# Two buffers for transposed rows, plain logits, held-back output scatters, and expert slots that start one unit later, in a convolution with routed experts

## The chip, the cores and the metric

The kernel runs on one core of one Trainium2 chip. The metric is the time on the device in microseconds (us).

## The reference, cut to what matters

```python
B, S, D, H, K = 8, 3584, 192, 8, 7           # 28672 rows of 192
N, E, F = B * S, 8, 1024
w = softmax(weight)                          # (H, K): one causal 7-tap filter per head
x = causal_conv(x, w).reshape(N, D)
logits = x @ w_gate                          # (N, E)
e_idx  = argmax(logits, axis=1)              # each row goes to one expert
gate_w = softmax(logits)[arange(N), e_idx]
eom    = sigmoid(x @ w_output_gate)
for e in range(E):
    mask = e_idx == e
    out[mask] = gate_w[mask, None] * eom[mask, e, None] * (relu(x[mask] @ w1[e]) @ w2[e])
```

## The kernel before

The rows are worked through in 16 units of 1792. A unit's front convolves the rows, computes 16 logits per row, picks an expert, and scatters the rows, pair by pair, into one stream per expert in DRAM. A slot is the expert work on 512 rows of one expert's stream: it is loaded with two transposing DMAs (xa, xb), multiplied with w1, put through a ReLU, multiplied with w2 and scattered to the output. While the slots of unit u run, in steps q = 0 to 3 each, generators `front_a(u + 2)` and `front_b(u + 1)` lay the fronts of later units between their products.

```python
pxt = ctx.enter_context(tc.tile_pool(name="pxt", bufs=6))       # xa, xb
...
NXS = 6                                                         # buffers of the stream scatters
...
# front_a: the logits, four products at a time in four column tiles
pl = pft()
for i in range(2):
    for g in range(4):
        nc.tensor.matmul(pl[32 * g:32 * g + 32, 0:4 * BT],
                         wg[:, (g // 2) * 2 + i, :],
                         tt[:, g // 2 + i, (g % 2) * 4 * BT:(g % 2 + 1) * 4 * BT],
                         start=(i == 0), stop=(i == 1), tile_position=(0, 32 * g))
...
def plan(u):                      # four slots a unit, of one half of the experts; eight in the last
    if u == 0:
        return []
    p = plan_half((u + 1) % 2, "a")
    if u == NU - 1:
        p += plan_half(u % 2, "b")
    return p
...
# Slot.second, at the end of each pair of steps: one stream scatter, then one output scatter
            for j in (q - 1, q):
                emit_in()
                i = nc.gpsimd.indirect_dma_start(out=out, out_offset=..., in_=self.y[:, j, :], ...)
...
for u in range(1, NU):            # main part
    todo = []
    for e, bap, inv in plans.pop(u):
        base = reg(bap, [ET.SP], E * CAP - TT)
        todo.append((e, inv, slot_load(base, u)))
    fa = front_a(u + 2) if u + 2 < NU else iter(())
    fb = front_b(u + 1) if u + 1 < NU else iter(())
    for k, (e, inv, xab) in enumerate(todo):
        s = Slot(xab, w_at(e * WE), inv)
        for q in range(4):
            s.first(q)
            drain(fa, 1)
            if prev is not None:
                prev.second(q)
            drain(fb, 1)
        prev = s
    ...
with tc.For_i(0, rn, 1):          # a loop takes what is left, one slot per turn
    ...
```

Of the kernel before, what the change touches and what calls it, by code (L numbers as in the profile page):

```python
# [11 lines left out]
FP16 = mybir.dt.float16  # L12
# [9 lines left out]
def kernel(  # L22
# [10 lines left out]
    nc = tc.nc  # L33
# [26 lines left out]
    WE = F + F + FCH * D  # L60
    BIG = float(1 << 30)
# [10 lines left out]
    pxt = ctx.enter_context(tc.tile_pool(name="pxt", bufs=6))  # L72
# [65 lines left out]
    wg = const.tile([128, 4, 32], FP32)  # L138
    nc.vector.memset(wg, 0.0)
    for i, (p0, p1, d0) in enumerate([(0, 128, 0), (0, 64, 128), (64, 128, 0), (0, 128, 64)]):  # L140
        nc.scalar.dma_start(wg[p0:p1, i, 0:E], moe_w_gate[d0:d0 + p1 - p0, :])
        nc.scalar.dma_start(wg[p0:p1, i, E:2 * E], moe_w_output_gate[d0:d0 + p1 - p0, :])
# [50 lines left out]
    NXS = 6  # L193
# [7 lines left out]
    nc.vector.tensor_copy(out=pos16, in_=poi.rearrange("p r j -> p (r j)"))  # L201

# [43 lines left out]

    wres = const.tile([128, E * WE], FP16)

    def load_w(e):
        o = e * WE  # L250
        nc.gpsimd.dma_start(wres[:, o:o + F], moe_w1[e, 0:128, :])
        nc.gpsimd.dma_start(wres[0:64, o + F:o + 2 * F], moe_w1[e, 128:D, :])
        nc.gpsimd.dma_start(
            wres[:, o + 2 * F:o + WE].rearrange("p (c d) -> p c d", d=D),
            moe_w2[e].rearrange("(c p) d -> p c d", p=128))

# [28 lines left out]
    def front_a(u):  # L285
# [12 lines left out]
        tt = pct.tile([128, 3, NB // 2 * BT], FP32, tag="tt", name="tt")  # L298
        cvf = cv.rearrange("p c d -> p (c d)")
        for g in range(6):  # L300
            pt = pft()
            for j in range(4):
                m, i = (g // 3) * 4 + j, g % 3
                nc.tensor.matmul(pt[:, j * BT:(j + 1) * BT],  # L304
                                 cvf[0:BT, m * 2 * D + i * 128:m * 2 * D + (i + 1) * 128],
                                 identf[0:BT, 0:BT],
                                 is_transpose=True, start=(j == 0), stop=(j == 3))
            evac(tt[:, g % 3, (g // 3) * 4 * BT:(g // 3 + 1) * 4 * BT], pt[:, 0:4 * BT])
            yield
        pl = pft()  # L310
        for i in range(2):
            for g in range(4):
                nc.tensor.matmul(pl[32 * g:32 * g + 32, 0:4 * BT],
                                 wg[:, (g // 2) * 2 + i, :],
                                 tt[:, g // 2 + i, (g % 2) * 4 * BT:(g % 2 + 1) * 4 * BT],
                                 start=(i == 0), stop=(i == 1), tile_position=(0, 32 * g))
        lt = pct.tile([128, 4 * BT], FP32, tag="lt", name="lt")
        evac(lt, pl[:, 0:4 * BT])
        yield
        pg = pft()  # L320
        for j in range(4):
            nc.tensor.matmul(pg[0:BT, j * 128:(j + 1) * 128],
                             lt[:, j * BT:(j + 1) * BT], identf,
                             is_transpose=True, start=(j == 0), stop=(j == 3))
        gb = pr.tile([128, NB, 16], FP32, tag="gb", name="gb")

        nc.vector.tensor_copy(
            out=gb[0:BT].rearrange("p (l i) e -> p i l e", l=2),
            in_=pg[0:BT].rearrange("p (i l e) -> p i l e", l=2, e=32)[:, :, :, 0:16])
# [140 lines left out]

    def nodep(i, group, others):
        inst = i.ins if hasattr(i, "ins") else i
        for o in others:
            tc.declare_no_dep(inst, group=o, reason="distinct rows of the stream or output")
        tc.add_to_no_dep_group(group, inst)
# [27 lines left out]

    def plan(u):
        if u == 0:
            return []
# [240 lines left out]
```

## Time and profile before

| | kernel before |
|---|---|
| timed runs | 806.73 us median of 3 (802.25 to 811.64) |
| profiled run | 773.92 us, span 772.0 |
| TensorE busy | 655.4 us, 85% of the span |
| TensorE waiting for the transposed load of a slot | 73.3 us |
| a full unit (first product of its first slot to that of the next unit) | 43.2 us |

The lines behind these numbers are shown in the prediction.

### The profile page before, as it was taken

How to read it: one execution, taken by the hardware profiler on the slowest of the kernel's cores; microseconds unless marked ns; L12 is line 12 of the kernel's file. 1: busy time of each engine (PE TensorE's matmuls, PEld its weight loads, DVE VectorE, ACT ScalarE, POOL GpSimd, SP SyncE). 2: the span in 40 equal slices, each digit the busy share in tenths (PEclk: the TensorE clock that was granted, in tenths of full speed). 3: DMA queues.
4: the chain of work that ended last, by engine and by line, in shares of the span. 5: the costliest groups of instructions: out<-in, count | busy, mean ns of one | idle time of the engine just before them, and what ended most of it. 6: DMA issues, size and time to landing. Idle time of an engine off the chain costs nothing. (4 is left out here: it accounts for less than half of the span.)

```text
span 772.0 us, 14134 instructions
## 1 busy us (share of the span) xinstructions
PE 655.4 (85%) x4948; PEld 436.2 (57%) x4948; DVE 406.5 (53%) x1298; ACT 366.5 (47%) x581; POOL 411.5 (53%) x425
## 2 busy tenths in 40 slices
PE   3866498989989898989989898989989898869953
PEld 1524165665757475656747475656757575547632
DVE  7425183836566383837556383837566474802220
ACT  0657153554535363545536364545546354436621
POOL 1436145473747465473737465563737375656652
PEclk9978599999999999999999999999999999989987
DMA  7999933253535343252535343442532313234110
GB/s 152 231 238 203 142 101 108 72 160 75 144 102 143 103 133 104 69 155 73 152 92 139 99 127 106 101 133 62 157 88 74 93 61 110 70 102 114 48 41 9
DMA packets 132359, 86.59 MB, mean 112 GB/s; under 512 B 88427, under 2 KB 122455, under 8 KB 132288
## 3 DMA queue, kind: packets, MB, share of 16 engines
q1 hardware_dynamic: 102656, 42.35, 23.4%
q0 software_dynamic: 28736, 43.31, 20.5%
q8 instruction: 39, 0.64, 0.4%
q14 instruction: 32, 0.26, 0.1%
q10 hardware_dynamic: 896, 0.03, 0.1%
HBM read 35.80 MB, written 44.43 MB: 104 GB/s over the span
## 5 line engine op out<-in xcount | busy, mean ns | idle before, releaser
L579 POOL DMA_INDIRECT out_dram<-y,oi x260 | 262.7, 1011 | 242.1 <-issue 179.0
L547 ACT ACTIVATE ht<-pp 128x1024 f16<-128x1024 f32 x195 | 199.3, 1022 | 183.9 <-PE pp L541 183.9
L539 PE MATMUL pp<-xa,wres 128*128 128x512 f16 x520 | 203.0, 390 | 61.1 <-DMA xa<-xcg_sorted 61.1
L558 PE MATMUL pyt<-wres,ht 128*128 128x192 f16 (+1 forms) x2080 | 220.9, 250 | 2.9 <-DVE ht L545 2.9
L558 PEld LDWEIGHTS <-ht 128*128 128x128 f16 x2080 | 182.7, 99 | 67.1 <-issue 37.0
L541 PE MATMUL pp<-xb,wres 128*128 128x512 f16 x520 | 202.2, 389 | 12.2 <-DMA xb<-xcg_sorted 12.2
L457 POOL DMA_INDIRECT xcg_sorted<-xs,du x128 | 130.1, 1017 | 89.4 <-ACT xs L278 42.2
L290 PE MATMUL pf<-xt,band 118*112 118x384 f32 x256 | 115.3, 543 | 19.5 <-DMA xt<-in_x_dram 14.1
L539 PEld LDWEIGHTS <-wres 128*128 128x128 f16 (+1 forms) x520 | 51.4, 99 | 112.4 <-DMA xa<-xcg_sorted 41.2
L545 DVE TENSOR_SCALAR ht<-pp 128x1024 f16<-128x1024 f32 x65 | 79.2, 1219 | 59.2 <-PE pp L541 59.2
L569 ACT COPY y<-pyt 128x384 f32<-128x384 f32 x130 | 62.4, 480 | 93.9 <-PE pyt L558 84.1
L280 DVE COPY cv<-pf 112x384 f32<-112x384 f32 x54 | 29.2, 541 | 89.3 <-PE pf L290 89.3
L290 PEld LDWEIGHTS pf<-xt,band 118*112 118x112 f32 x256 | 48.0, 195 | 48.9 <-DVE band L133 13.6
L541 PEld LDWEIGHTS <-wres 128*128 128x128 f16 (+1 forms) x520 | 51.8, 100 | 37.6 <-issue 8.2
L572 DVE TENSOR_SCALAR oi<-pyt 128x4 uint32<-128x4 f32 x65 | 10.5, 162 | 115.8 <-ACT y L569 110.3
L439 PE MATMUL pf<-xrow,pm 112*128 112x194 f16 x512 | 64.6, 247 | 6.9 <-DVE pm L423 4.5
L418 DVE TENSOR_TENSOR xrow<-cv,gs 112x384 f16<-112x384 f32 x128 | 64.7, 545 | 0.0
L423 DVE TENSOR_SCALAR pm<-pos,pos 112x256 f16<-112x256 f16 x256 | 64.6, 324 | 0.0
L304 PEld LDWEIGHTS pf<-identf,cv 112*128 112x128 f32 x384 | 43.6, 141 | 17.4 <-DVE cv L280 2.2
L278 ACT COPY cv<-pf 112x384 f32<-112x384 f32 x74 | 33.9, 479 | 40.1 <-PE pf L290 25.0
L304 PE MATMUL pf<-identf,cv 112*128 112x112 f32 x384 | 51.5, 260 | 0.5 <-ACT cv L278 0.4
L278 ACT CAST xs<-pf 128x388 f16<-128x388 f32 x76 | 37.2, 489 | 28.8 <-PE pf L439 20.2
(132 smaller groups left out, 425.0 us busy)
## 6 DMA issues: line engine op xcount, KB each, us to landing
xt<-in_x_dram SPq DMA_DIRECT2D x8, 1344.0 KB
xt<-in_x_dram SPq DMA_DIRECT2D x8, 1260.0 KB
out_dram<-y,oi POOLq DMA_INDIRECT x260, 2.7
wres<-in_moe_w_dram POOLq DMA_DIRECT2D x8, 384.0 KB, 10.5
wres<-in_moe_w_dram POOLq DMA_DIRECT2D x8, 256.0 KB, 11.5
xcg_sorted<-zrow SPq DMA_DIRECT2D x8, 256.0 KB
xcg_sorted<-xs,du POOLq DMA_INDIRECT x128, 3.2
xa<-xcg_sorted SPq DMA_TRANSPOSE x65
```

The lines of the kernel that those rows point to most:

```text
L278: nc.scalar.copy(out=o, in_=i)
L290: nc.tensor.matmul(pc[0:BT, 0:NB * GH], band[0:KI, h, :], xt[0:KI, :, h * GH:(h + 1) * GH], start=True, stop=True)
L304: nc.tensor.matmul(pt[:, j * BT:(j + 1) * BT], cvf[0:BT, m * 2 * D + i * 128:m * 2 * D + (i + 1) * 128], identf[0:BT, 0:BT], is_transpose= ...
L418: nc.vector.tensor_tensor(out=xr[P, k:k + 2, 0:D], in0=cv[P, k:k + 2, :], in1=gs[P, k:k + 2].unsqueeze(2).to_broadcast([BT, 2, D]), op=ALU ...
L423: nc.vector.tensor_scalar(out=pms[i][P, l, :], in0=pos16[P], scalar1=pos[P, l * NG + i:l * NG + i + 1], scalar2=None, op0=ALU.is_equal)
L457: i = nc.gpsimd.indirect_dma_start(out=xcg2, out_offset=bass.IndirectOffsetOnAxis(ap=du[:, i:i + 1], axis=0), in_=xs.rearrange("p r w -> p ...
L539: nc.tensor.matmul(pp[:, j, :], self.w(fc * 128, 128), self.xa, start=True, stop=False)
L541: nc.tensor.matmul(pp[:, j, :], self.w(F + fc * 128, 128), self.xb, start=False, stop=True)
L545: nc.vector.tensor_relu(out=ht, in_=pp)
L547: nc.scalar.activation(out=ht, in_=pp, func=AF.Relu)
L558: nc.tensor.matmul(self.pp[:, o:o + D], self.ht[fc // 2][:, fc % 2, q * 128:(q + 1) * 128], self.w(2 * F + fc * D, D), start=(fc == 0 and ...
L579: i = nc.gpsimd.indirect_dma_start(out=out, out_offset=bass.IndirectOffsetOnAxis(ap=self.oi[:, j:j + 1], axis=0), in_=self.y[:, j, :], in_ ...
```

## The change

The intent: take away the wait for the load at every unit's start by sending the stream scatters at once and holding the output scatters back; shorten the end by replacing the loop with three slots of the fullest experts; and simplify two things that seemed to have slack (buffers, logits). Beside the core of the diff below, the expert weights are loaded two experts at a time along the front-only units, and the two halves of the experts change places in `plan`. The core:

```diff
-    pxt = ctx.enter_context(tc.tile_pool(name="pxt", bufs=6))
+    pxt = ctx.enter_context(tc.tile_pool(name="pxt", bufs=2))
-    NXS = 6
+    NXS = 12
...
-        for i in range(2):
-            for g in range(4):
-                nc.tensor.matmul(pl[32 * g:32 * g + 32, 0:4 * BT], ..., tile_position=(0, 32 * g))
...
+        for hh in range(2):
+            ...
+            for i in range(3):
+                nc.tensor.matmul(pl[0:32, 0:4 * BT], wg[:, i, :], tt[:, i, cs],
+                                 start=(i == 0), stop=(i == 2))
+            evac(lt[:, cs], pl[0:32, 0:4 * BT])
+        for m in range(NG):                    # eight transposes of 32 rows for four of 128
+            nc.tensor.matmul(pg[0:BT, m * 32:(m + 1) * 32], lt[:, m * BT:(m + 1) * BT],
+                             identf[0:32, 0:32], is_transpose=True, ...)
...
+    U0 = 2
-        if u == 0:
+        if u < U0:
             return []
...
-                for j in (q - 1, q):
-                    emit_in()
-                    i = nc.gpsimd.indirect_dma_start(out=out, ...)
+                pout.extend((self.y, self.oi, j) for j in (q - 1, q))
...
-    for u in range(1, NU):
+    for u in range(U0, NU):
...
+        if u == NU - 1:
+            for sel, bap, inv in [pick() for _ in range(ND)]:      # ND = 3
+                base = reg(bap[0:1, 0:1], [ET.SP], E * CAP - TT)
+                todo.append((sel, inv, slot_load(base, u)))
...
-                drain(fb, 1)
+                live = drain(fb, 1)
+                pos = 4 * k + q
+                emit_in(len(pend))
+                emit_out(5 if live and pos > 3 else 0)
```

More of the change, by code (lines that the diff above doesn't have):

```diff
@@ L60 @@
     WE = F + F + FCH * D
+    ND = 3
     BIG = float(1 << 30)
@@ L136 @@
                 data=cw[:, h:h + H // 2, k:k + 1].to_broadcast([128, H // 2, BT]))
-    wg = const.tile([128, 4, 32], FP32)
+    wg = const.tile([128, 3, 32], FP32)
     nc.vector.memset(wg, 0.0)
-    for i, (p0, p1, d0) in enumerate([(0, 128, 0), (0, 64, 128), (64, 128, 0), (0, 128, 64)]):
-        nc.scalar.dma_start(wg[p0:p1, i, 0:E], moe_w_gate[d0:d0 + p1 - p0, :])
-        nc.scalar.dma_start(wg[p0:p1, i, E:2 * E], moe_w_output_gate[d0:d0 + p1 - p0, :])
+    for i, c, p0, p1, d0 in ((0, 0, 0, 128, 0), (1, 0, 0, 64, 128), (1, 16, 64, 128, 0),
+                             (2, 16, 0, 128, 64)):
+        nc.scalar.dma_start(wg[p0:p1, i, c:c + E], moe_w_gate[d0:d0 + p1 - p0, :])
+        nc.scalar.dma_start(wg[p0:p1, i, c + E:c + 2 * E], moe_w_output_gate[d0:d0 + p1 - p0, :])
     ltri = const.tile([128, 128], FP16)
@@ L201, with load_w @@
     nc.vector.tensor_copy(out=pos16, in_=poi.rearrange("p r j -> p (r j)"))
+    wres = const.tile([128, E * WE], FP16)
+    def load_w(e):
+        o = e * WE
+        nc.gpsimd.dma_start(wres[:, o:o + F], moe_w1[e, 0:128, :])
+        nc.gpsimd.dma_start(wres[0:64, o + F:o + 2 * F], moe_w1[e, 128:D, :])
+        nc.gpsimd.dma_start(
+            wres[:, o + 2 * F:o + WE].rearrange("p (c d) -> p c d", d=D),
+            moe_w2[e].rearrange("(c p) d -> p c d", p=128))
+    load_w(0)
     GE = NG * E
@@ L244 @@
     nc.vector.memset(zrow, 0.0)
-    wres = const.tile([128, E * WE], FP16)
-    def load_w(e):
-        o = e * WE
-        nc.gpsimd.dma_start(wres[:, o:o + F], moe_w1[e, 0:128, :])
-        nc.gpsimd.dma_start(wres[0:64, o + F:o + 2 * F], moe_w1[e, 128:D, :])
-        nc.gpsimd.dma_start(
-            wres[:, o + 2 * F:o + WE].rearrange("p (c d) -> p c d", d=D),
-            moe_w2[e].rearrange("(c p) d -> p c d", p=128))
     def zero_w(e):
@@ L298, in front_a @@
         tt = pct.tile([128, 3, NB // 2 * BT], FP32, tag="tt", name="tt")
+        lt = pct.tile([32, NB // 2 * BT], FP32, tag="lt", name="lt")
         cvf = cv.rearrange("p c d -> p (c d)")
-        for g in range(6):
-            pt = pft()
-            for j in range(4):
-                m, i = (g // 3) * 4 + j, g % 3
-                nc.tensor.matmul(pt[:, j * BT:(j + 1) * BT],
-                                 cvf[0:BT, m * 2 * D + i * 128:m * 2 * D + (i + 1) * 128],
-                                 identf[0:BT, 0:BT],
-                                 is_transpose=True, start=(j == 0), stop=(j == 3))
-            evac(tt[:, g % 3, (g // 3) * 4 * BT:(g // 3 + 1) * 4 * BT], pt[:, 0:4 * BT])
-            yield
@@ L310, in front_a @@
-        pl = pft()
-        for i in range(2):
-            for g in range(4):
-                nc.tensor.matmul(pl[32 * g:32 * g + 32, 0:4 * BT],
-                                 wg[:, (g // 2) * 2 + i, :],
-                                 tt[:, g // 2 + i, (g % 2) * 4 * BT:(g % 2 + 1) * 4 * BT],
-                                 start=(i == 0), stop=(i == 1), tile_position=(0, 32 * g))
-        lt = pct.tile([128, 4 * BT], FP32, tag="lt", name="lt")
-        evac(lt, pl[:, 0:4 * BT])
-        yield
+        for hh in range(2):
+            cs = slice(hh * 4 * BT, (hh + 1) * 4 * BT)
+            for i in range(3):
+                pt = pft()
+                for j in range(4):
+                    o = (hh * 4 + j) * 2 * D + i * 128
+                    nc.tensor.matmul(pt[:, j * BT:(j + 1) * BT], cvf[0:BT, o:o + 128],
+                                     identf[0:BT, 0:BT],
+                                     is_transpose=True, start=(j == 0), stop=(j == 3))
+                evac(tt[:, i, cs], pt[:, 0:4 * BT])
+                if not (hh == 1 and i == 1):
+                    yield
+            pl = pft()
+            for i in range(3):
+                nc.tensor.matmul(pl[0:32, 0:4 * BT], wg[:, i, :], tt[:, i, cs],
+                                 start=(i == 0), stop=(i == 2))
+            evac(lt[:, cs], pl[0:32, 0:4 * BT])
+            yield
@@ L320, in front_a @@
         pg = pft()
-        for j in range(4):
-            nc.tensor.matmul(pg[0:BT, j * 128:(j + 1) * 128],
-                             lt[:, j * BT:(j + 1) * BT], identf,
-                             is_transpose=True, start=(j == 0), stop=(j == 3))
+        for m in range(NG):
+            nc.tensor.matmul(pg[0:BT, m * 32:(m + 1) * 32], lt[:, m * BT:(m + 1) * BT],
+                             identf[0:32, 0:32],
+                             is_transpose=True, start=(m == 0), stop=(m == NG - 1))
@@ L325, in front_a @@
         gb = pr.tile([128, NB, 16], FP32, tag="gb", name="gb")
-        nc.vector.tensor_copy(
-            out=gb[0:BT].rearrange("p (l i) e -> p i l e", l=2),
-            in_=pg[0:BT].rearrange("p (i l e) -> p i l e", l=2, e=32)[:, :, :, 0:16])
+        nc.vector.tensor_copy(out=gb[0:BT],
+                              in_=pg[0:BT, 0:NB * 16].rearrange("p (c e) -> p c e", e=16))
         units[u] = cv, gb
@@ L469, in emit_in, with emit_out @@
             n -= 1
+    pout = deque()
+    def emit_out(keep=0):
+        while len(pout) > keep:
+            y, oi, j = pout.popleft()
+            i = nc.gpsimd.indirect_dma_start(
+                out=out, out_offset=bass.IndirectOffsetOnAxis(ap=oi[:, j:j + 1], axis=0),
+                in_=y[:, j, :], in_offset=None, bounds_check=N - 1, oob_is_err=False)
+            nodep(i, "out", ("out",))
+            last[0] = "out"
     def nodep(i, group, others):
@@ L502, in plan_half, with pick @@
         return [(e0 + i, bu[0:1, i:i + 1], iu[:, i, :]) for i in range(EH)]
+    U0 = 2
     def plan(u):
-        if u == 0:
+        if u < U0:
             return []
-        p = plan_half((u + 1) % 2, "a")
+        p = plan_half(u % 2, "a")
         if u == NU - 1:
-            p += plan_half(u % 2, "b")
+            p += plan_half((u + 1) % 2, "b")
         return p
+    def pick():
+        lv = pr.tile([128, E], FP32, tag="lv", name="lv")
+        nc.vector.tensor_tensor(out=lv, in0=R, in1=DN, op=ALU.subtract)
+        lm = pr.tile([128, 1], FP32, tag="lm", name="lm")
+        nc.vector.tensor_reduce(out=lm, in_=lv, axis=AX.X, op=ALU.max)
+        oh = pr.tile([128, E], FP32, tag="oh", name="oh")
+        nc.vector.scalar_tensor_tensor(out=oh, in0=lv, scalar=lm, in1=rev,
+                                       op0=ALU.is_equal, op1=ALU.mult)
+        om = pr.tile([128, 1], FP32, tag="om", name="om")
+        nc.vector.tensor_reduce(out=om, in_=oh, axis=AX.X, op=ALU.max)
+        sel = pr.tile([128, 1], U32, tag="sel", name="sel", bufs=ND)
+        nc.vector.tensor_scalar(out=sel, in0=om, scalar1=-float(WE), scalar2=float(E * WE),
+                                op0=ALU.mult, op1=ALU.add)
+        nc.vector.tensor_scalar(out=oh, in0=oh, scalar1=om, scalar2=None, op0=ALU.is_equal)
+        bt = pr.tile([128, E], FP32, tag="bt", name="bt")
+        nc.vector.scalar_tensor_tensor(out=bt, in0=R, scalar=-float(TP), in1=DN,
+                                       op0=ALU.add, op1=ALU.min)
+        nc.vector.scalar_tensor_tensor(out=bt, in0=bt, scalar=2.0, in1=oh,
+                                       op0=ALU.mult, op1=ALU.mult)
+        bo = pr.tile([128, 1], FP32, tag="bo", name="bo")
+        nc.vector.tensor_reduce(out=bo, in_=bt, axis=AX.X, op=ALU.add)
+        bou = pr.tile([128, 1], U32, tag="bou", name="bou", bufs=ND)
+        nc.vector.tensor_copy(out=bou, in_=bo)
+        tk1 = pr.tile([128, 1], FP32, tag="tk1", name="tk1")
+        nc.vector.tensor_scalar(out=tk1, in0=lm, scalar1=float(TP), scalar2=None, op0=ALU.min)
+        nc.vector.scalar_tensor_tensor(out=DN, in0=oh, scalar=tk1, in1=DN,
+                                       op0=ALU.mult, op1=ALU.add)
+        nc.vector.tensor_scalar(out=tk1, in0=tk1, scalar1=-2.0, scalar2=float(TT),
+                                op0=ALU.mult, op1=ALU.add)
+        iv1 = pr.tile([128, 4], FP32, tag="iv1", name="iv1")
+        nc.vector.tensor_scalar(out=iv1, in0=rowf, scalar1=tk1, scalar2=BIG,
+                                op0=ALU.is_lt, op1=ALU.mult)
+        iu1 = pr.tile([128, 4], U32, tag="iu1", name="iu1", bufs=ND)
+        nc.vector.tensor_copy(out=iu1, in_=iv1)
+        return sel, bou, iu1
@@ L576, in second @@
                                             op=ALU.bitwise_or)
-                for j in (q - 1, q):
-                    emit_in()
-                    i = nc.gpsimd.indirect_dma_start(
-                        out=out, out_offset=bass.IndirectOffsetOnAxis(
-                            ap=self.oi[:, j:j + 1], axis=0),
-                        in_=self.y[:, j, :], in_offset=None,
-                        bounds_check=N - 1, oob_is_err=False)
-                    nodep(i, "out", ("out",))
-                    last[0] = "out"
+                pout.extend((self.y, self.oi, j) for j in (q - 1, q))
     def reg(ap, engines, hi):
@@ L609, in chain @@
             yield from g
-    for e in range(EH):
-        load_w(e)
+    load_w(1)
     drain(front_a(0))
     ze = 0
-    for u in range(2):
+    for u in range(U0 + 1):
         fa, fb = front_a(u + 1), front_b(u)
@@ L626 @@
         emit_in(len(pend))
-        if u == 0:
-            for e in range(EH, EH + 2):
-                load_w(e)
+        if u < U0:
+            load_w(2 + 2 * u)
+            load_w(3 + 2 * u)
     while ze < E:
@@ L639 @@
             base = reg(bap, [ET.SP], E * CAP - TT)
-            todo.append((e, inv, slot_load(base, u)))
+            todo.append((w_at(e * WE), inv, slot_load(base, u)))
+        if u == NU - 1:
+            for sel, bap, inv in [pick() for _ in range(ND)]:
+                base = reg(bap[0:1, 0:1], [ET.SP], E * CAP - TT)
+                todo.append((sel, inv, slot_load(base, u)))
         fa = front_a(u + 2) if u + 2 < NU else iter(())
         fb = front_b(u + 1) if u + 1 < NU else iter(())
-        for k, (e, inv, xab) in enumerate(todo):
-            if u == 1 and k < 2:
-                load_w(EH + 2 + k)
-            s = Slot(xab, w_at(e * WE), inv)
+        for k, (w, inv, xab) in enumerate(todo):
+            if u == U0 and k < 2:
+                load_w(E - 2 + k)
+            if not callable(w):
+                w = w_dyn(reg(w[0:1, 0:1], [ET.PE], (E - 1) * WE))
+            s = Slot(xab, w, inv)
             for q in range(4):
@@ L658 @@
         prev.second(q)
+        emit_out()
     lf = const.tile([128, E], FP32)
@@ L676 @@
     with tc.For_i(0, rn, 1):
-        lv = pr.tile([128, E], FP32, tag="lv", name="lv")
-        nc.vector.tensor_tensor(out=lv, in0=R, in1=DN, op=ALU.subtract)
-        lm = pr.tile([128, 1], FP32, tag="lm", name="lm")
-        nc.vector.tensor_reduce(out=lm, in_=lv, axis=AX.X, op=ALU.max)
-        oh = pr.tile([128, E], FP32, tag="oh", name="oh")
-        nc.vector.scalar_tensor_tensor(out=oh, in0=lv, scalar=lm, in1=rev,
-                                       op0=ALU.is_equal, op1=ALU.mult)
-        om = pr.tile([128, 1], FP32, tag="om", name="om")
-        nc.vector.tensor_reduce(out=om, in_=oh, axis=AX.X, op=ALU.max)
-        sel = pr.tile([128, 1], U32, tag="sel", name="sel")
-        nc.vector.tensor_scalar(out=sel, in0=om, scalar1=-float(WE), scalar2=float(E * WE),
-                                op0=ALU.mult, op1=ALU.add)
-        nc.vector.tensor_scalar(out=oh, in0=oh, scalar1=om, scalar2=None, op0=ALU.is_equal)
-        bt = pr.tile([128, E], FP32, tag="bt", name="bt")
-        nc.vector.scalar_tensor_tensor(out=bt, in0=R, scalar=-float(TP), in1=DN,
-                                       op0=ALU.add, op1=ALU.min)
-        nc.vector.scalar_tensor_tensor(out=bt, in0=bt, scalar=2.0, in1=oh,
-                                       op0=ALU.mult, op1=ALU.mult)
-        bo = pr.tile([128, 1], FP32, tag="bo", name="bo")
-        nc.vector.tensor_reduce(out=bo, in_=bt, axis=AX.X, op=ALU.add)
-        bou = pr.tile([128, 1], U32, tag="bou", name="bou")
-        nc.vector.tensor_copy(out=bou, in_=bo)
-        tk1 = pr.tile([128, 1], FP32, tag="tk1", name="tk1")
-        nc.vector.tensor_scalar(out=tk1, in0=lm, scalar1=float(TP), scalar2=None, op0=ALU.min)
-        nc.vector.scalar_tensor_tensor(out=DN, in0=oh, scalar=tk1, in1=DN,
-                                       op0=ALU.mult, op1=ALU.add)
-        nc.vector.tensor_scalar(out=tk1, in0=tk1, scalar1=-2.0, scalar2=float(TT),
-                                op0=ALU.mult, op1=ALU.add)
-        iv1 = pr.tile([128, 4], FP32, tag="iv1", name="iv1")
-        nc.vector.tensor_scalar(out=iv1, in0=rowf, scalar1=tk1, scalar2=BIG,
-                                op0=ALU.is_lt, op1=ALU.mult)
-        iu1 = pr.tile([128, 4], U32, tag="iu1", name="iu1")
-        nc.vector.tensor_copy(out=iu1, in_=iv1)
+        sel, bou, iu1 = pick()
         base = reg(bou[0:1, 0:1], [ET.SP], E * CAP - TT)
@@ L716 @@
             s.second(q)
+            emit_out()
 _INS = ['x', 'weight', 'moe_w_gate', 'moe_w_output_gate', 'moe_w1', 'moe_w2']
```

## The prediction

> **What bounds the kernel now.** I read the page first, then the table of stretches cut at the stages, then the waits, then the order of time around one stage boundary.
>
> The first view is the page, engine totals and the slices of the span.
>
> ```profile
> PE 655.4 (85%) x4948; PEld 436.2 (57%) x4948; DVE 406.5 (53%) x1298; ACT 366.5 (47%) x581; POOL 411.5 (53%) x425
> PE   3866498989989898989989898989989898869953
> PEclk9978599999999999999999999999999999989987
> ```
>
> TensorE is at 8 to 9 tenths from slice 6 to slice 38 and loses time at both ends; no other engine passes 53%. The chain of waits has only the last output scatter in it, so it doesn't help. The second view is the table of stretches (columns: length, busy time and count for PE, PEld, DVE, ACT, POOL, granted clock, DMA share, GB/s).
>
> ```profile
> 28.40:47.90 19.50, 14.57 (x101) 8.87 (x99) 13.70 (x52) 11.83 (x25) 6.67 (x7) 1.00 1.20 254
> 47.90:75.90 28.00, 19.32 (x98) 10.30 (x98) 11.98 (x50) 17.48 (x33) 14.15 (x17) 0.76 1.00 223
> 86.10:129.90 43.80, 38.05 (x270) 24.05 (x271) 26.47 (x81) 20.23 (x31) 19.87 (x20) 0.92 0.50 114
> 216.90:259.10 42.20, 38.67 (x307) 26.33 (x307) 23.35 (x73) 21.34 (x34) 24.57 (x25) 1.00 0.43 119
> 647.60:687.30 39.70, 29.20 (x247) 20.07 (x248) 20.41 (x72) 17.77 (x26) 24.31 (x25) 0.96 0.30 90
> 687.30:742.10 54.80, 54.16 (x452) 37.64 (x452) 13.06 (x29) 31.82 (x41) 31.12 (x33) 0.97 0.30 76
> 742.10:772.00 29.90, 10.65 (x52) 5.26 (x52) 4.78 (x23) 4.50 (x6) 8.45 (x9) 0.73 0.09 24
> ```
>
> The first two rows are the front-only units (no expert products yet), the second of them slow. The third is the first unit with slots (a slot: 512 rows of one expert). The fourth is a typical unit at full clock: 38.67 us of TensorE work in 42.2 us, so about 3.5 us of idle. Then come the unit with half of the front, the last eight slots, and the loop at the end: 29.9 us with 10.65 of TensorE work, for a single slot. The thirteen units from 86.1 to 647.6 take (647.6 - 86.1)/13 = 43.2 us each. The third view, the waits, says what the idle is.
>
> ```profile
> PE pp L539 <- DMA xa<-xcg_sorted: 61.1, 16, 13.4
> PE pp L541 <- DMA xb<-xcg_sorted: 12.2, 16, 2.5
> SPq L516 <- DMA xcg_sorted<-xs,du: 253.0, 32, 20.2
> ```
>
> 73.3 us of the 116.6 us that TensorE is idle are waits for the transposed load of a stage's first slot, and that load waits for the stage's scatters. The fourth view is TensorE in order of time at one boundary, the fifth GpSimd at the same place.
>
> ```profile
> 122.96 1.71 PE L313 MATMUL pf<-tt,wg 128*32 128x448 f32 x16
> 124.61 0.83 PE L558 MATMUL pyt<-wres,ht 128*128 128x192 f16 x8
> 126.14 0.60 PE L322 MATMUL pf<-identf,lt 128*112 128x128 f32 x4
> 126.58 0.82 PE L558 MATMUL pyt<-wres,ht 128*128 128x192 f16 x8
> 129.93 0.38 PE L539 MATMUL pp<-xa,wres 128*128 128x512 f16 x1 [2.53 <-DMA xa<-xcg_sorted]
> 130.77 0.38 PE L541 MATMUL pp<-xb,wres 128*128 128x512 f16 x1 [0.46 <-DMA xb<-xcg_sorted]
> ```
>
> ```profile
> 122.78 0.98 POOL L579 DMA_INDIRECT out_dram<-y,oi  x1 [0.30 <-issue]
> 124.07 0.98 POOL L457 DMA_INDIRECT xcg_sorted<-xs,du  x1 [0.30 <-issue]
> 125.36 0.98 POOL L579 DMA_INDIRECT out_dram<-y,oi  x1 [0.30 <-issue]
> ```
>
> The last product for the sorted stream ends at 118.2, yet its scatter is issued at 124.07: inputs and outputs alternate on GpSimd at 1.29 us each, and it is some 5 us behind. The load follows at 126.58 and TensorE starts at 129.93.
>
> [...] 16 half-products of 448 columns take 124.61 - 122.96 = 1.65 us, while a convolution pair of 384 columns takes 0.65 us alone (0.32 each). [...] after the wait for a load, products spaced 0.216 us come 0.43 us apart for up to 3.4 us, and some units show a mean clock of 0.96, others 1.00. [...] Here it is 126.58 - 124.07 = 2.5 us from a scatter's issue to the load that waits for it.
>
> **The change, part by part.** All times are in the span of the profile; the scaling comes last.
>
> *Logits.* Before: 8 products in 4 column tiles, 1.65 us per unit. After: 6 products, each in two halves, one after the other: 12 x 0.32 x 448/384 = 4.5 us. The transposes of the result become 8 of 32 rows for 4 of 128: with 0.11 us each now (0.44 for 4), and some 0.10 for the fp32 weight load, 0.8 us. Together +3.2 us of TensorE per unit. In the full units TensorE is the bound, so it is on the path.
>
> *Outputs held back.* While a front still produces scatters, up to five outputs stay queued and every input goes out at once. From the last product (step 12 of 16) to the next unit's first slot TensorE then has 4 x 1.53 (first and second products of a step) + 0.1 + 0.4 + 0.8 + 2.3 + 0.8 = 10.5 us. The chain beside it: copy 0.7, GpSimd free 0.7, scatter to load 2.5, load to first product 3.35 (126.58 to 129.93), and 0.85 to the second operand: 8.1 us. It fits with 2 us to spare. So the 3.5 us of idle and the half clock behind it (43.2 - 42.2 = 1.0 us on average) go.
>
> *Two buffers.* A slot's second operand is read last at the second step of the following slot, and only then may the load of the slot after that start. With fronts beside it there are over 4 us left, against 2.9 us from issue to use (127.87 to 130.77). In bare slots, 6.2 us each (first product at 690.81, the next slot's same one at 697.00), about 3.0 us are left: no margin. I take 1 us in all there.
>
> A full unit: 38.67 + 3.2 + 0.2 = 42.1 us, against 43.2. So what the waits give, the logits mostly take back.
>
> *One more front-only unit, one fewer with slots.* The first front is done at 28.4 now; +2.5 for the logits makes 31. A front-only unit took 19.5 us, of which 2.3 were a wait for x, and 28 us in the second, which shows a clock of 0.76, the same late x, and a copy that waits 7.4 us for one of six scatter buffers. With twelve buffers and the weights spread (two experts ahead instead of four) I expect 20.5 us each with the logits: 31 + 61.5 = 92.5. From the last product to the first slot it was 86.1 - 72.7 = 13.4 us, beside 3 MB of weights that are there again; less lag on GpSimd gives 12.5. So the first slot comes at 105 instead of 86.1. Its unit pays the late second operand (2.5) and a cold clock (4), and lacks 2.6 of second products: 46.
>
> *Slots.* I counted the experts' rows per unit from the inputs and followed both schedules. Before, 64 slots are laid out and one expert has 108 pairs left: one turn of the loop. After, 60 and three picks of 104, 102 and 82 pairs: nothing is left, the loop turns zero times. 63 slots instead of 65.
>
> *The end.* The half-front unit: 28.6 us of work, 3.5 us of VectorE waits that stay (1.03, 1.23, 0.64, 0.55), and 2.5 of load wait instead of 6.9: 34.6. The last unit has 11 slots: 54.8 + 3 x 6.2 = 73.4, minus 1 for a warmer start. The three picks are 45 small VectorE instructions ahead of the first slot's ReLU, 2.8 us per pick (744.13 to 746.9): VectorE is free at 8.5, the ReLU ready near 10.2 where TensorE needs it at 7.5: +2.7. Reading the weight offset into TensorE's registers and register-addressed operands: +4, a guess from the loop's slower second products. With the buffers' 1: 80.1. After TensorE's end: outputs lagged 4.8 us, the last takes 1, and 6.1 passed from the last output to the end of the span: 13 instead of 29.9.
>
> Sum: 105 + 46 + 11 x 42.1 + 34.6 + 80.1 + 13 = 742 us, against 772.0: 3.9% less. The timed runs before lie above the profiled one, 806.73 to 773.92, which nothing in the trace explains; I assume the same factor 1.042: **774 us**.
>
> **The rivals.** (a) The load wait stays: the x load now queues behind the fourth slot's load (it needs a buffer), so 1.3 MB go out just when the last scatters do. Against it: x is asked for at step 10, so should be gone by step 14. If 3 us of wait per unit remain, +36 us: 778 in the profile, 811 timed, no gain. (b) Two buffers bind in all slots: half a microsecond in each of 63 adds 30 us[...]. For it: no margin in the last unit; against: 4 us or more elsewhere. (c) The logits hide: if TensorE has slack left in the full units (VectorE chain, copies), the 3.2 us cost less; then 42.1 becomes 40 and the sum 719, timed 750. Against it: 38.67 of 42.2 is dense work. (d) Front-only units run at half clock as the second does: +8 us each, 25 in all, timed 800.
>
> **Range and chances.** The sum's weak terms are the start (8 us either way), the unit (1 us times 12) and the last unit (5): about 16 us together, and the timed runs spread by 1.2%. So 750 to 796. Under 790.6 is faster by 2%: 0.75. Within 2%: 0.22, mostly (a) or (d). Slower: 0.03.
>
> **What would show it.** Right: one unit near 42 us at clock 1.00 with the wait for xa nearly gone; logits 4.5 us per unit; the first slot near 105; no loop slot; 11 slots at 6.2 to 6.6. Wrong: waits for xa or xb in most slots, front-only units of 28 us, a long stop of TensorE at the picks, or timed runs that don't keep the factor 1.042.

## The result, and the profile after

| | before | changed | ratio |
|---|---|---|---|
| the first comparison | 808.34 us median of 4 (802.25 to 811.64) | 862.89 us median of 4 (861.14 to 866.77) | 1.069 [1.061, 1.077] |
| chip 9, later | 779.74 us median of 8 (776.54 to 785.81) | 741.57 us median of 4 (739.50 to 745.48) | 0.952 [0.945, 0.958] |

The changed kernel is 6.9% slower in the first comparison and 4.8% faster on chip 9. Both are the same program, and both pairs ran side by side. The second row is the experiment `after_again` below; its profile belongs next to the first, because the difference between the two is the subject.

The page of the changed kernel, first comparison:

```profile
span 860.6 us, 14061 instructions
PE 710.6 (83%) x4844; PEld 446.6 (52%) x4844; DVE 401.5 (47%) x1314; ACT 366.2 (43%) x593; POOL 407.0 (47%) x417
PE   2988479897979969697996969799796988678884
PEclk9899779998999989899998989989897999989998
```

The page of the same kernel on chip 9:

```profile
span 737.8 us, 14061 instructions
PE 676.6 (92%) x4844; PEld 429.5 (58%) x4844; DVE 403.5 (55%) x1314; ACT 365.8 (50%) x593; POOL 400.7 (54%) x417
PE   3897919999999999999999999999999999989994
```

On chip 9 TensorE is at 9 tenths from slice 7 nearly to the end, which is what the change was for. In the first comparison about every second slice falls to 6 or 7. Next the stretches (columns as in the prediction: length, then busy time and count for PE, PEld, DVE, ACT and POOL, the granted clock, DMA share, GB/s). First comparison: the front-only units, a full unit, a full unit whose front loads no x, and six slots of the last unit.

```profile
33.67:93.38 59.71, 52.02 (x279) 28.18 (x279) 35.61 (x141) 39.62 (x82) 29.88 (x32) 0.97 0.77 157
160.21:209.42 49.21, 43.87 (x308) 28.17 (x306) 26.02 (x79) 21.25 (x34) 24.70 (x24) 0.95 0.37 102
612.51:664.20 51.69, 44.68 (x309) 28.66 (x307) 25.31 (x80) 21.36 (x34) 24.64 (x24) 0.90 0.24 68
781.84:826.37 44.53, 38.77 (x315) 25.84 (x313) 8.39 (x18) 23.06 (x30) 23.52 (x24) 1.00 0.27 74
```

Chip 9, the same stages:

```profile
30.84:90.51 59.67, 52.05 (x279) 28.17 (x278) 35.24 (x141) 39.75 (x82) 29.82 (x32) 0.97 0.82 171
151.76:193.81 42.05, 41.73 (x308) 26.97 (x307) 25.28 (x79) 21.22 (x34) 23.79 (x25) 1.00 0.44 120
572.23:614.27 42.04, 41.72 (x308) 26.95 (x307) 25.35 (x79) 21.22 (x34) 23.66 (x25) 1.00 0.29 84
668.26:706.38 38.12, 37.33 (x316) 25.80 (x313) 9.30 (x19) 23.50 (x30) 23.40 (x25) 1.00 0.39 86
```

What TensorE waits for longest changes with it (total us, times, longest us). In the first comparison:

```profile
PE pf L326 <- DVE lt L285: 47.1, 8, 6.8
PE pp L592 <- DMA xa<-xcg_sorted: 12.2, 1, 12.2
```

On chip 9 the waits of L326 add to 1.1 us, and those for xa to 14.2 us in 2 places.

The front-only units, with the heaviest transfers of all (DMA share 0.77 and 0.82), take the same time to 0.04 us. The full units, with the same instructions, take 7 to 10 us more in the first comparison, and the slots 44.53 / 6 = 7.4 us each instead of 6.4. The order of time at the end of one full unit says how. First comparison, TensorE, then VectorE, then ScalarE:

```profile
197.16 0.24 PE L618 MATMUL pyt<-idw,xb 128*128 128x1 f16 x4
...
197.91 0.38 PE L594 MATMUL pp<-xb,wres 128*128 128x512 f16 x1
198.22 2.44 PE L320 MATMUL pf<-tt,wg 128*32 128x448 f32 x6
...
202.22 0.40 PE L326 MATMUL pf<-identf,lt 32*112 32x32 f32 x4
207.66 0.58 PE L326 MATMUL pf<-identf,lt 32*112 32x32 f32 x4 [5.03 <-issue]
```

```profile
206.99 0.61 DVE L285 COPY lt<-pf 32x448 f32<-32x448 f32 x1 [4.91 <-remote]
```

```profile
201.21 0.48 ACT L622 COPY y<-pyt 128x384 f32<-128x384 f32 x1 [3.77 <-PE pf L320]
202.75 1.02 ACT L600 ACTIVATE ht<-pp 128x1024 f16<-128x1024 f32 x1 [1.07 <-PE pp L594]
```

The same place on chip 9:

```profile
187.53 0.24 PE L618 MATMUL pyt<-idw,xb 128*128 128x1 f16 x4
...
188.28 0.38 PE L594 MATMUL pp<-xb,wres 128*128 128x512 f16 x1
188.58 2.44 PE L320 MATMUL pf<-tt,wg 128*32 128x448 f32 x6
...
192.59 0.62 PE L326 MATMUL pf<-identf,lt 32*112 32x32 f32 x8
```

```profile
191.06 0.61 DVE L285 COPY lt<-pf 32x448 f32<-32x448 f32 x1 [2.39 <-PE pf L320]
```

Read it along one dependence. On chip 9 the copy of the second half of the logits (L285 on VectorE) starts at 191.06, just after the six logit halves that began at 188.58 with a length of 2.44. In the first comparison they began at 198.22, so should end at 200.66, but the copy starts at 206.99: 6.3 us later, with VectorE idle. ScalarE sees the same: its copy of y waits for the signal of L618, the last products into the tile that it reads, recorded from 197.16 to 197.40, and starts at 201.21. (The line puts this wait down to L320, whose recorded start is nearer; the semaphore record that fits L618 lies at 201.19.) TensorE then runs out of work (5.03 us) and restarts at half clock (granted from 206.98 for 6.8 us), the second half of the loss.

The trace also records semaphore updates. I matched TensorE's updates, in order, with the ends of the instructions that make them. In the profile of the kernel before, all 840 pairs lie within 0.07 us. In the changed kernel on chip 9 all come within 0.02 us and at most 2 of 900 have no record. In the first comparison some 5% come 6 us late or more, the latest 11 us, and 86 have no record (where records are missing the matching can slip by one; the largest was checked against ScalarE, whose ReLU after a product recorded to 744.91 starts at 755.79). I call this a **late signal**. TensorE's recorded starts there run ahead of what its consumers can use. So a product's recorded end and its signal are two different things: in this profile they are up to 11 us apart.

### The profile page after: what moved, and what is told of

It reads as the page before. It is cut to its first block, busy times and chain, and to the rows that moved or that the text cites. A ratio compares the mean times of both kernels' runs of the same rounds, so it can differ in the third digit from the quotient of the medians. Undisturbed runs are those within 1.5% of the kernel's fastest.

```text
span 860.6 us, 14061 instructions
## 1 busy us (share of the span) xinstructions
PE 710.6 (83%) x4844; PEld 446.6 (52%) x4844; DVE 401.5 (47%) x1314; ACT 366.2 (43%) x593; POOL 407.0 (47%) x417
## 3 DMA queue, kind: packets, MB, share of 16 engines
q0 software_dynamic: 28352, 43.31, 18.4%
## 5 line engine op out<-in xcount | busy, mean ns | idle before, releaser
L479 POOL DMA_INDIRECT out_dram<-y,oi x252 | 247.8, 983 | 228.5 <-issue 116.9
L600 ACT ACTIVATE ht<-pp 128x1024 f16<-128x1024 f32 x189 | 193.4, 1024 | 181.5 <-PE pp L594 144.9
L459 POOL DMA_INDIRECT xcg_sorted<-xs,du x128 | 140.5, 1097 | 204.9 <-DVE xs L285 147.5
L592 PE MATMUL pp<-xa,wres 128*128 128x512 f16 x504 | 198.9, 395 | 26.6 <-ACT ht L600 12.3
L594 PE MATMUL pp<-xb,wres 128*128 128x512 f16 x504 | 198.1, 393 | 7.4 <-DMA xb<-xcg_sorted 6.9
L598 DVE TENSOR_SCALAR ht<-pp 128x1024 f16<-128x1024 f32 x63 | 76.8, 1218 | 27.6 <-remote 10.4
L320 PE MATMUL pf<-tt,wg 128*32 128x448 f32 x192 | 80.1, 553 | 2.0 <-ACT tt L283 1.1
L285 DVE CAST xs<-pf 128x388 f16<-128x388 f32 x100 | 55.8, 558 | 34.0 <-PE pf L441 27.6
L326 PE MATMUL pf<-identf,lt 32*112 32x32 f32 x128 | 14.6, 239 | 67.6 <-DVE lt L285 47.1
L283 ACT COPY cv<-pf 112x384 f32<-112x384 f32 x104 | 48.0, 479 | 44.1 <-PE pf L295 27.8
L441 PEld LDWEIGHTS <-pm 112*128 112x128 f16 x512 | 41.8, 97 | 23.4 <-DVE pm L425 15.7
```

The lines of the kernel that those rows point to most:

```text
L320: nc.tensor.matmul(pl[0:32, 0:4 * BT], wg[:, i, :], tt[:, i, cs], start=(i == 0), stop=(i == 2))
L441: nc.tensor.matmul(ps[:, r * XW:(r + 1) * XW], pm[P, l, r * 128:(r + 1) * 128], xr[P, l * NG + i, :], start=(r == 0 and l == 0), stop=(r = ...
L459: i = nc.gpsimd.indirect_dma_start(out=xcg2, out_offset=bass.IndirectOffsetOnAxis(ap=du[:, i:i + 1], axis=0), in_=xs.rearrange("p r w -> p ...
L479: i = nc.gpsimd.indirect_dma_start(out=out, out_offset=bass.IndirectOffsetOnAxis(ap=oi[:, j:j + 1], axis=0), in_=y[:, j, :], in_offset=Non ...
L592: nc.tensor.matmul(pp[:, j, :], self.w(fc * 128, 128), self.xa, start=True, stop=False)
L594: nc.tensor.matmul(pp[:, j, :], self.w(F + fc * 128, 128), self.xb, start=False, stop=True)
```

## The experiments

"Chip kind" below means what the kernel before takes on it: about 807 us (the first comparison, chips 0 and 2) or about 778 us (chips 9 and 3). I could not choose the chip; each group of runs shared one.

### Undoing parts of the change (chip 0; the kernel before there 806.59 us)

Theories 1, 2 and 3 blame, for the late signals, the two buffers, the plain logits and the burst of held-back outputs.

**a_6buf**: changed kernel, `pxt` with `bufs=6`.

> The changed kernel with six buffers for the transposed rows again, nothing else. Theory 1 (two buffers: the load of a slot is now issued in the middle of a slot, when TensorE signals the last read of a buffer, and the late signals at the end of every unit hang on it): the full unit falls from 50 to about 42 us and the time to 775-790. Theory 2 (the plain logits cost it): stays at 850-865. Theory 3 (the burst of held-back output scatters on GpSimd costs it): stays at 850-865.

Measured: 865.23 us, ratio 1.072 [1.069, 1.075]. Nothing gained. Theory 1 falls: the buffers are not the cause.

**b_2buf**: kernel before, `pxt` with `bufs=2`.

> The kernel before with two buffers instead of six, nothing else. Theory 1: the units grow by some 5 us and the time by 60 or more, to 860-880, with TensorE's signals late as in the changed kernel. Theories 2 and 3: the time stays within 10 us of 808, because the kernel before has neither the plain logits nor the held-back outputs.

Measured: 820.89 us, 1.019 [1.015, 1.022]. The late signals are there, up to some 6 us in the units, in a kernel that has only the buffers of the change. (Near the end of the program they reach 8 us.) That fits none of the three as I had stated them, and was the first hint that the kernel is not what brings them. The kernel before itself has no profile on a chip of this kind; this run is its nearest relative there.

**a_tiled**: changed kernel, the logits in column tiles again.

```diff
-                nc.tensor.matmul(pl[0:32, 0:4 * BT], wg[:, i, :], tt[:, i, cs], ...)
+                nc.tensor.matmul(pl[32 * g:32 * g + 32, 0:4 * BT], ..., tile_position=(0, 32 * g))
```

> The changed kernel with the logits in four column tiles again, two buffers and the rest kept. Theory 2 (the plain logits and their 32-row transposes cost more than the 3.2 us per unit that I had counted): falls to 790 or less. Theories 1 and 3: falls by 3.2 us for each of some 14 units, about 40 us at most, to 820-860, and the stop of TensorE near the end of every unit (4 to 6 us) stays.

Measured: 817.10 us, 1.014 [1.011, 1.018]: 46 us less than the changed kernel in the first comparison (48 less than a_6buf on this chip), late signals up to 11 us still there. Near theories 1 and 3's figure: the term of the logits, about 3 us in each of 16 units, not more. A kernel that has lost its plain logits and waits hardly for loads is still 1.4% slower than the kernel before, on this chip.

**a_nohold**: changed kernel, outputs not held back.

```diff
-                emit_out(5 if live and pos > 3 else 0)
+                # all pending inputs and outputs go out in this step, taking turns
```

> The changed kernel with inputs and outputs alternating on GpSimd as in the kernel before, no output held back. Theory 3: the burst of nine outputs at the end of each unit goes, and with it the late signals: 780-800. Theories 1 and 2: no gain; the load wait of 3-4 us per unit comes back, so 860-900.

Measured: 841.35 us, 1.044 [1.041, 1.048]; late signals of 4 to 6 us, once 9, at other places of the unit. My edit was not what I had announced: in the kernel before an input waits for a later step's output, here it goes out in its own step. So it undoes the holding back only, and the load wait did not come back. Theory 3 falls too: without a burst the signals are late all the same. But the time fits no theory either: without the holding back the kernel is 22 us faster on this kind of chip, where on chip 9 the holding back gains 28 us (a_slots to a_best, below). The same edit, though in versions with other buffers and logits, has opposite signs on the two kinds.

### The kernel before again, and the parts one by one (chip 9; the kernel before there 779.77 us)

The expectations of this group were written in the belief that the chip would be like the one before, at 807 us.

**b_again**: the kernel before, unchanged, for its profile.

> The kernel before once more, unchanged, for its profile only: the profile that the prediction was made from showed 774 us, while all eleven timed runs lie between 802 and 812. Theory A (that profile caught a rare run; the usual run has TensorE's signals late at the unit ends, as every experiment so far has): the profile shows 802-812, full units of 45 us instead of 43.2, and late signals of 2 to 6 us. Theory B (the profile is right and the changed kernel alone has late signals): the profile shows no late signals.

Measured: 776.43 us; no late signal (0.07 us at most), waits for xa 62.9 us where the first profile had 61.1. So neither theory A nor B as written: the profile that the prediction used is not a rare run, it is the usual run of another chip. That is an inference (the first profile carries no chip number), but span, waits, signals and the number of semaphore records in the trace (12212 and 12200; the six profiles of slow chips hold at most 7862) all agree, and no run of this kernel on a chip of the other kind came under 802 us.

**b_hold**: kernel before, outputs held back, each input sent in its step, twelve scatter buffers. **b_hold2**, **b_hold3** and **b_hold4** are the same program.

> The kernel before with outputs held back and twelve scatter buffers. Prediction's own step (the load wait of 4.5 us per unit goes): 750-770. Theory 3 (the burst of outputs at each unit's end makes TensorE's signals late): 815-830.

> The kernel before with only the outputs held back, once more, for another chip. On a chip like 9: 710 again. On a chip like 0, if TensorE is held up there whenever it is dense: 770-800, little of the 9% left; if not: 735, the same 9%.

> The kernel before with only the outputs held back, once more. On a chip like 9: 710. On a chip like 0: by theory E 785-807, as the waits taken away come back as hold-ups; by theory F 735-750, the 70 us stay a gain.

> The kernel before with only the outputs held back, once more, hoping for a chip like 0 or 2, where the kernel before takes 806. There, by theory E in the form that the paced kernel left (TensorE is held up wherever its work is over some 82% of the time, as 41.5 us of work in units of 50): units of 38.2 / 0.82 = 46.5 us, as the kernel before has there or longer, and 800-820, no gain. If the hold-ups belong to the plain logits or to the two buffers instead: 735-750. On a chip like 9: 711 again.

Measured: 710.02, 711.16 and 712.13 us on chip 9 (ratio 0.909 [0.904, 0.915] in the first) and 709.64 on chip 3. I was hoping for a chip of the slow kind and got none, so what this version does there is open. A full unit of the kernel before and one of b_hold, on chip 9:

```profile
217.60:261.40 43.80, 40.32 (x307) 27.13 (x306) 23.35 (x73) 21.45 (x34) 24.41 (x25) 0.96 0.42 114
```

```profile
202.80:241.40 38.60, 38.29 (x308) 26.38 (x307) 24.68 (x79) 21.36 (x34) 23.99 (x24) 1.00 0.49 129
```

The idle time and the half clock go, as the prediction's ledger says: 4.5 us of a unit (on average 43.0 to 38.5).

**a_slots**: changed kernel with six buffers, column tiles, outputs not held back.

> The changed kernel with six buffers, the logits in column tiles and outputs not held back: only the change of the slots (from the third unit on, three last) is left. If the parts add: 863 - 46 (column tiles) - 21 (not held back) = 796, and 785-790 if the six buffers give their 14 us here as in the kernel before. If the slots are the true loss: above 810.

Measured: 716.56 us, 0.918 [0.913, 0.924]. The edit has a_nohold's flaw: inputs still go out at once. The true undo is **b_slots**, the kernel before with only the new slots:

> The kernel before with only the slots changed (from the third unit on, three for the fullest experts last); six buffers, column tiles, outputs and inputs alternating as before. By the ledger: one turn of the loop less (-17 us at the end), start +19, one unit of slots fewer (-43) and three slots more in the last unit (+25): 760-770 on a chip like 9, a gain of 1 to 2%; on a chip like 0 790-805.

Measured (chip 9): 756.06 us, 0.972 [0.963, 0.980]: 24 us gained, somewhat more than I had expected (four runs from 750 to 763 us, the longest of them slow; whether it is 2% stays just open). The 39.5 us between b_slots and a_slots are then what sending the inputs at once gives, with twelve scatter buffers; holding the outputs back adds 28 us more (a_slots to a_best below).

**b_plain** and **b_plain2**: kernel before, plain logits only.

> The kernel before with only the logits changed to plain products. The term of my prediction, 2.85 to 3.2 us in each of 16 units, gives 46-51: 852-858. If the load wait of each unit swallows part of it (the kernel before waits 4.5 us per unit for its loads): 820-840.

> The kernel before with only the plain logits, once more. On a chip like 9: 780, the waits for the loads swallow the 4.5 us per unit. On a chip like 0: by theory E 835-860, because there the dense TensorE, not the load wait, sets the time, and 2.85 us or more are added in 16 units; by theory F 805-820.

Measured: 779.90 us both times, on chip 9, 0.999 [0.993, 1.006]. On this kind of chip the logits cost nothing in the kernel before: the waits for xa fall from 62.9 to 32.8 us in the same time. The same products cost 31 us in the changed kernel (a_tiled2 below), whose full units hardly wait for loads.

### The changed kernel on chip 9, and the version that is best there

**after_again**: the changed kernel, unchanged.

> The changed kernel once more, unchanged. By now two chips have shown themselves: on chip 0 the kernel before takes 807 us and every kernel with a dense TensorE shows late signals; on chip 9 it takes 780 and no kernel shows any. Theory C (the loss is TensorE being held up on the one chip, which the ledger didn't have): on a chip like 9, 745-765, so 2 to 4% faster than before and near the ledger's 742 for the profile; on a chip like 0, 863 again. Theory D (something in the changed kernel itself costs it, wherever it runs): 835 or more on both.

Measured: 741.57 us, 0.952 [0.945, 0.958], span 737.8, no late signals. Theory C, and a little better than it asked.

**a_best**: changed kernel, six buffers, column tiles.

> The changed kernel with six buffers and the logits in column tiles; held-back outputs and the new slots kept. On a chip like 9: the 710 of the held-back outputs less 5 to 15 us for the slots, 695-712. On a chip like 0: 805-820, as with column tiles and two buffers, because late signals eat the gain.

Measured: 688.17 us, 0.883 [0.877, 0.889]. It beats both kernels on chip 9, by 11.7% and 7.2%. Its unit has no idle time left:

```profile
217.20:255.30 38.10, 38.10 (x310) 26.40 (x308) 25.27 (x79) 21.12 (x33) 24.71 (x25) 1.00 0.50 131
```

It was not run on a chip of the slow kind; its nearest relative there is a_tiled.

**a_tiled2**: a_tiled once more.

> The changed kernel with the logits in column tiles, two buffers kept, once more. On a chip like 0: 817 again. On a chip like 9: 690-697, because two buffers cost no more there than the 1 us of the ledger to some 0.5 us per unit over the 688 with six buffers.

Measured (chip 9): 710.66 us, 0.912 [0.906, 0.918], against 817.10 on chip 0. My 690 to 697 was wrong: two buffers cost 22 us beside a_best, and TensorE waits 19.5 us for xa and 13.3 for xb. In the changed kernel the logits cover these waits: adding them back takes only 741.57 - 710.66 = 31 us.

### Is TensorE held up because it is dense?

**a_paced**: changed kernel with one PSUM buffer for the first products, so that each waits for the ReLU of the one before. It also ran as **a_paced2**.

```diff
-    ps_h = ctx.enter_context(tc.tile_pool(name="ps_h", bufs=2, space=bass.MemoryType.PSUM))
+    ps_h = ctx.enter_context(tc.tile_pool(name="ps_h", bufs=1, space=bass.MemoryType.PSUM))
```

> The changed kernel with one PSUM buffer for the first products instead of two, so that TensorE has to wait for the ReLU in each step and is idle a good part of the time. Theory E (on chip 0 TensorE is held up because it is dense): on a chip like 0 no late signals are left, a bare slot of the last unit takes 7.5-8.5 us as it does on a chip like 9, and both kinds of chip agree within 2%. Theory F (the hold-ups come from the transfers beside it, dense or not): on a chip like 0 the late signals of 2-6 us stay and each slot is over 1 us longer than on a chip like 9.

> The paced kernel once more, hoping for a chip like 0. There, by theory E (held up because dense): 790-810, the 792 of chip 9 within 2%, no late signals, bare slots of 8.9 us as on chip 9. By theory F (held up by the transfers): 840 or more, late signals of 2 us and over. On a chip like 9: 792 again.

Measured: 792.42 us on chip 9 (1.016 [1.007, 1.024]) and 900.15 us on chip 2 (1.117 [1.112, 1.122]). By my own yardstick of total time this is theory F. But the stages say more. Six slots of the last unit, chip 9 and then chip 2:

```profile
705.60:759.30 53.70, 41.02 (x313) 26.38 (x312) 9.30 (x18) 23.50 (x30) 23.54 (x24) 1.00 0.23 62
```

```profile
823.20:877.00 53.80, 41.95 (x313) 26.67 (x313) 9.29 (x18) 23.61 (x30) 23.53 (x24) 1.00 0.24 57
```

In these slots the pacing bites (8.95 us a slot instead of 6.4), and the chips agree within 0.1 us; in these slots I find no late signal. Without the pacing the slots of the slow kind took 7.4 us. In the full units the pacing hardly bites (43.4 us on chip 9 instead of 42.05, because the fronts fill the gaps), and there chip 2 takes 51.7 us on average with signals 4 to 8 us late. So with the same transfers the hold-up goes where TensorE's work is thinned, and stays where it isn't. The pacing thins everything that TensorE sets off as well, its signals and records among it, so this does not say which of them counts. And the transfers alone don't bring it: the front-only units have the most of them (DMA share 0.77) and lose nothing, and units without an x load (DMA share 0.24 instead of 0.37) lose as much as those with one.

**What stays open** is what in these chips holds the signals up. Two things fit. First, a limit on TensorE's work: it gets through 42.05 us of work in 50.24, 1.19 times as long. Against it: the granted clock recorded in the first comparison is 1.0 or 0.5 and nothing between, its six bare slots took 44.53 us where chip 9 took 38.12, both at a granted clock of 1.00, and products of 512 columns still start 0.21 us apart (197.70 and 197.91). This program has one core; what the other cores of those chips did is not known. (The recorded starts run up to 11 us ahead of what consumers can use, so their spacing alone says little of the rate at which products finish.) And the same work per full unit takes 48.3 us in a_nohold, 50.2 in the changed kernel and 51.7 in the paced one on chips of this kind, so it is no fixed rate of work. Second, a limit on signals or records: the full unit has 753 instructions in 42.05 us, 17.9 per us, and 15.3 per us on the slow kind; the six bare slots 18.4 and 15.7; the stretches without late signals only 13.6 (front-only units) and 13.0 (paced slots). The late signals most often begin at L618, four one-column products 0.03 us apart; they then come out in rows 0.03 to 0.06 us apart, closer than the products they belong to; and records are missing (86 of 900 in the first comparison). That the path of signals and records can hold TensorE up is my guess: no run here shows it doing so, so this is a candidate and not a finding. Every run also carries a record of its clock, so I can't say whether the hold-up exists where nothing is recorded.

A count of what the traces hold speaks for the second. Both profiles of the changed kernel have all 14061 instructions, but 7334 semaphore records in the first comparison and 11972 on chip 9. All six profiles of the slow kind have 6958 to 7862, all fourteen of the fast kind 11531 to 12223, kernels as dense as a_best and b_hold among them. Instructions and semaphore records together come to 24.5 per us in the full units of the first comparison, 27.0 in the six bare slots and 26.6 in the front-only units; on chip 9 to 36.4, 39.3 and 29.4. So on the slow kind about the same number of records comes out in a microsecond, whatever the stage. It is no proof: in the paced slots of chip 2 records are missing too (24.3 per us, 28.0 on chip 9), and no signal is late there. Nor is it shown that the chip is what differs: chips 0 and 2 were each seen in one group of runs alone, so their state at that hour would fit as well.

## Why the prediction was wrong

The ledger of spans, against both kinds of chip:

| term | predicted | chip 9 | first comparison |
|---|---|---|---|
| first slot begins | 105 | 107.4 | 109.4 |
| its unit | 46 | 44.4 | 50.8 |
| a full unit, 11 times | 42.1 | 42.05 | 50.24 |
| half-front unit | 34.6 | 33.8 | 44.0 |
| last unit and tail | 80.1 + 13 = 93.1 | 89.7 | 103.7 |
| span | 742 | 737.8 | 860.6 |

The ledger was made from a profile of the fast kind, and on that kind it is right to 0.6%, each term within 3.5 us. Some of that is luck: the misses add to 8.8 us, in both directions, and cancel to 4. The tail's parts as written (4.8, 1 and 6.1) make 11.9 us and not 13; it measured 10.4, and the last unit 79.3.

- **The step that failed** is the last: the timed runs "lie above the profiled one, 806.73 to 773.92, which nothing in the trace explains; I assume the same factor 1.042". The gap was not a factor. As far as the record goes, it was the mark of a second kind of chip, on which signals of a dense TensorE come late (by up to 11 us); that the profile came from the fast kind is inferred (b_again), and why the slow kind holds signals up stays open. There the kernel before, which idles 3.5 us in each unit, loses 3.5% (807 to 780), while the changed kernel, which hardly idles (41.73 us busy of 42.05), loses 16% (863 to 742). Of the 119 us between 742 and 860.6, the full units are 11 x 8.1 = 90. What a_tiled gains in density on the fast kind it gives back on the slow one, and more: it gains 69 us on chip 9 and loses 11 on chip 0.
- **The load wait goes**: right on both. The wait for xa is 12.2 us in the first comparison, one wait, from 61.1. b_hold shows the size: 43.2 to 38.6 us a unit.
- **Logits +3.2 us a unit**: right to half a microsecond. The changed unit of 42.05 us stands against 38.4 in a_best, 3.7 more; six halves take 2.44 us each time, twice a unit. That they hide behind waits (rival c) is what the kernel before does with them (b_plain), and not the changed kernel.
- **Two buffers, 1 us in all**: right for the changed kernel on the fast kind (4.8 us of waits for xb in five places), but only because the logits make room; with column tiles they cost 22 us.
- **The slots and the end**: right within 4 us; no turn of the loop was left, as counted.
- **The half clock goes with the wait**: right on chip 9, where the full units shown were granted 1.00. In the profile that the prediction read, half clock at the unit boundaries came after waits of 2.5 to 3.0 us (2.53 at 129.93) and lasted 3.4 us; what it calls a cold clock is the 0.92 granted in the first unit with slots. In the first comparison half clock comes with the hold-ups instead (5.03 us of idle, then 6.8 us from 206.98).
- **Rivals**: (a) and (b) didn't occur as told, nor did (d): on both kinds the front-only units took 59.7 us, where 61.5 was predicted. A rival was missing that asks whether the profile and the times were taken on like machines. "Timed runs that don't keep the factor 1.042" stood in the last paragraph as a way to be wrong, and carried only a 3% chance of slower.

## What to carry to other kernels

Before building on a profile, compare its own time with the timed runs; if they differ by more than the runs among themselves, find out why first, because the profile may describe another machine. A change that only makes one engine denser should be judged on more than one chip: here the kernel before took 774 to 786 us on chips 9 and 3 and 802 to 812 on chips 0 and 2 and in the first comparison, but the denser changed kernel 742 and 863. And when a consumer starts us after its producer's recorded end (here up to 11), look at the semaphore's record, not at the busy time.
